# Two loads for the twiddle tables of a Fourier stage, and single moves in a written-out order

## The chip, the cores and the metric

The kernel runs on one core of one Trainium2 chip. The core has a matrix engine (TensorE, PE in the profile, with its weight loads as PEld), three engines for elementwise work (VectorE or DVE, ScalarE or ACT, GpSimd or POOL), and SyncE (SP), which here does little else than issue the transfers between the device's memory (DRAM) and the core's memory (SBUF). Matmul results are left in a third memory, PSUM, and are copied from there. The metric is the time of one execution on the device, in microseconds, as the median of several runs.

## The reference

One input x of 2048 rows and 640 columns goes through two computations, A and B, and a gate mixes them row by row:

```
g = sigmoid((x * gate_w).sum(-1, keepdims=True))
return g * A(x) + (1 - g) * B(x)
```

A is attention with a memory. There are 32 heads of 20 columns, and the rows are cut into four segments of 512. Inside a segment each head does ordinary causal softmax attention. Beside it the head reads a memory matrix M and a sum z, both built from the keys and values of earlier segments, with phi(t) = t + 1 for positive t and exp(t) otherwise:

```
a_mem = (phi(q) @ M) / (phi(q) . z + 1e-6)
o = sigmoid(beta) * a_mem + (1 - sigmoid(beta)) * softmax(q k^T * scale + mask) @ v
M = M + phi(k)^T @ v ;  z = z + phi(k).sum(rows)
```

The outputs of all heads are multiplied with wo. B is a filter in the frequency domain: a two-dimensional real Fourier transform of x, a product with the complex table w_r + 1j * w_i, and the inverse transform.

## The kernel before

The kernel is a Python program that first records operations and then places them. An operation is a group of matmuls, one elementwise instruction or one transfer, with the buffers that it reads and writes and, in some cases, a choice of two engines. The order of all operations is written out by hand as one long list of numbers, ORDER: half of a number (rounded down) is the operation, and an odd number picks the second engine of its choice. The function schedule cuts the list into one queue for each engine, keeps that order, and gives out the PSUM banks; emit then writes the instructions, with a wait on a semaphore wherever an operation needs what another engine has written, or overwrites what another engine still reads. An engine works off its queue strictly in order, so an operation that waits holds up everything behind it. The table QUEUE holds planned costs of transfers; it says nothing of when they really run.

Nearly all transfers are issued by SyncE, one after another, at line 602 (plain) and line 600 (transposing). Matmuls are issued at lines 565 and 567, and copies out of PSUM at lines 577 (ScalarE) and 579 (VectorE). A transfer that waits stands in SyncE's queue as an operation stands in an engine's.

The steps that matter for the change:

- **xT, ld_x.** xT is the transposed x of a segment, a transposing load that is needed by the projections; ld_x loads plain x for the Fourier stage, where VectorE and GpSimd add and subtract halves of it first (fold, tiles xf and xsb).
- **Projections.** proj and vproj multiply xT with wq, wk and wv. Their results are copied to SBUF (ev_proj, ev_v). As a head has only 20 columns, q and k are laid out anew for the score matmuls: st_qk writes them (tile qu) to a scratch tensor qk_scr in DRAM, and pad (in the first segment pad2, in eight smaller pieces) reads them back with gaps into the tile qkp.
- **Attention.** qk (score matmuls, from qkp), exp on ScalarE (line 1357), mask on GpSimd (line 1391), pvf and pv (products with v, tile va). The results go through tiles ub and the scratch tensor u_scr (st_u, ld_u).
- **Memory.** phi of k is computed (tile phk), and a transposing transfer from SBUF to SBUF, pkT, makes the tile pkn from it, which mupd uses to update M.
- **Fourier stage.** F1 is a first transform along the rows (tile Ac); D a transform along the columns (with the table big, copied to the tile Bt by ev_D); then for each of 16 groups g come T, the forward twiddle matmuls (line 1547), W_mul, the product with the filter on VectorE (line 1548, tile Pt), W_add on VectorE or GpSimd (line 1553, tile Yt), and Tb, the inverse twiddle matmuls (line 1568), copied to the tile Cp by ev_Tb. Last come Db and Fb for the inverse transforms. The filter rows are loaded by ld_W (tile Wt), the twiddles by ld_tt (tile tt).
- **End.** final (copies to the tile ot) mixes both computations; st_out and, for the last rows, four smaller st_part write the output.

The twiddle tiles are two, tt0 and tt1, each of 128 partitions and 2048 columns. Each holds the tables of two groups, a pair: of every 1024 columns the first 512 are read by T and the other 512 by Tb. The table in DRAM has the same layout. At every even g one transfer loads a pair:

```
self.dma(lambda tt=self.tt[ti]: tt.ap(0, [1024, 2], [1, 1024]), ...,
         2 * P * 2048, [], [b("tt", ti)], early, name="ld_tt")
```

As both T and Tb name the one buffer b("tt", ti), the load of pair k waits until the last Tb of pair k - 2 is done, and T of pair k waits for the whole load. There are eight such loads. After the Fourier stage the tiles' room is used again for others; after_mid lists the buffers that must be free by then.

TensorE works the array in three shapes: the whole array (projections, Fourier stage), tiles of 20 rows by 64 columns (qk), and tiles of 128 rows by 32 columns (pv, vproj in part, the output product). Along TensorE's queue the shape changes 206 times.

Of the kernel before, what the change touches and what calls it, by code (L numbers as in the profile page):

```python
# [510 lines left out]
class Kern:  # L511
# [84 lines left out]
    def dma(self, dst, src, nbytes, r, w, prio, tr=False, name="", after=(), queue="sp"):  # L596
# [24 lines left out]
        ("ld_big", 329728): (500.0, 950.0, 16, 1000.0), "ld_inv": (500.0, 1400.0, 16, 1000.0), ("ld_tt", 262144): (400.0, 1300.0, 16, 250.0), ("ld_tt", 524288): (400.0, 1750.0, 16, 600.0),  # L621
# [218 lines left out]
    def after_mid(self, key):  # L840

        if key in self.seen:
            return []
        self.seen.add(key)
        b = self.b
        return ([b("tt", i) for i in range(self.NT)] + [b("Wt", i, r, h) for i in range(2) for r in range(2) for h in range(2)] +
                [b("Bt", i, r) for i in range(2) for r in range(2)] + [b("Yt", i, r) for i in range(2) for r in range(2)] +
                [b("Pt", i, r, q) for i in range(2) for r in range(2) for q in range(2)])

# [878 lines left out]
```

## Time and profile before

| What | us |
|---|---|
| median of 3 runs (lowest, highest) | 234.89 (234.76, 235.56) |
| the profiled execution | 236.6 |
| its span | 234.5 |
| TensorE busy | 225.3 |
| VectorE busy | 190.0 |
| ScalarE busy | 194.6 |
| GpSimd busy | 148.3 |

The span is the time from the first to the last instruction on the core; the execution has 2.1 us around it. The granted clock of TensorE is full in all slices of the profile. Matmuls are pipelined and the ends that the profile gives for them are modelled, so a TensorE that is busy is not thereby at its best; what can be read well is when each matmul starts.

A row of a list of waits names the waiting engine and line, then behind the arrow who released it, and then the total of the waits, how many there were and the longest, in us. A row of a chain or of a timeline begins with a start and a length in us. SPq is SyncE issuing a transfer: its length is the time that the issue took, not the transfer, which lands later. A row of a tile gives the shortest, median and longest duration in ns and the first and the last start in us.

### The profile page before, as it was taken

The page shows a single profiled execution, that of the slowest core. Times are in us where ns is not written, and L with a number is a line of the kernel's source. Part 1 is how long each engine was busy: PE and PEld are TensorE (multiplying, and loading weights), DVE is VectorE, ACT ScalarE, POOL GpSimd, SP SyncE. Part 2 cuts the span into 40 slices and gives each one's busy share as a digit, 9 for nine tenths or more (in the row PEclk, how much of TensorE's full clock was granted, in tenths as well). Part 3 has the DMA queues.
Part 4 walks back from the last instruction along what each step waited for, and adds up shares of the span by engine and source line. Part 5 has one row for each costly group of instructions (what it writes and reads, how often), then busy time and mean ns, then how long its engine had stood idle before and what let it go on. Part 6 is the DMA issues. An engine that isn't in the chain of part 4 may idle for free.

```text
span 234.5 us, 10377 instructions
## 1 busy us (share of the span) xinstructions
PE 225.3 (96%) x4395; PEld 141.9 (61%) x4395; DVE 190.0 (81%) x485; ACT 194.6 (83%) x216; POOL 148.3 (63%) x301
## 2 busy tenths in 40 slices
PE   7899999999999999999999999999999998999994
PEld 2575576676547666654557555555645466767793
DVE  0189897889999998799999898999799983955364
ACT  2189797789999999999999989999999898788720
POOL 8233127456768875567775869478998768387700
PEclk9999999999999999999999999999999999999999
DMA  7999955998989978556893755685899752222524
GB/s 149 279 338 209 251 165 142 192 234 219 259 200 188 193 192 243 140 157 180 217 210 95 241 173 130 190 194 182 227 166 196 203 152 81 76 77 59 180 95 122
DMA packets 59265, 42.18 MB, mean 180 GB/s; under 512 B 30228, under 2 KB 55380, under 8 KB 59220
## 3 DMA queue, kind: packets, MB, share of 16 engines
q1 hardware_dynamic: 58180, 40.96, 70.3%
q8 instruction: 34, 0.56, 1.1%
q10 hardware_dynamic: 1040, 0.57, 1.0%
q14 instruction: 11, 0.09, 0.2%
HBM read 23.32 MB, written 12.30 MB: 152 GB/s over the span
## 4 chain that ended last, share of the span: by engine, by line
PE 69%; DVE 10%; DMA 8%; ACT 5%; SPq 4%; issue 2%; POOL 1%; DVEq 0%; ACTq 0%
PE psum L567 64%; PE psum L565 5%; DMA out_dram<-ot 4%; SPq L602 4%; ACT ex L1357 3%; DVE Pt L1548 3%; DMA xT<-in_A_x_dram 2%; DMA qk_scr<-qu 1%; DVE Cp L579 1%; DVE G L1602 1%; ACT ub L577 1%; DVE Bt L579 1%; DVE Yt L1553 1%; POOL ex L1391 1%; POOL Yt L1553 1%
## 5 line engine op out<-in xcount | busy, mean ns | idle before, releaser
L1357 ACT ACTIVATE ex<-psum 128x2048 bf16<-128x2048 f32 (+1 forms) x73 | 135.2, 1853 | 10.7 <-PE psum L567 9.5
L1391 POOL TENSOR_SCALAR_AFFINE_SELECT ex<-ex 128x256 bf16<-128x256 bf16 (+3 forms) x224 | 104.5, 484 | 42.0 <-ACT ex L1357 10.9
L567 PE MATMUL psum<-xT,wk 128*128 128x256 bf16 (+1 forms) x280 | 33.3, 273 | 0.2 <-DVE mem L1229 0.2
L567 PE MATMUL psum<-qkp 20*64 20x64 bf16 (+5 forms) x1280 | 31.9, 270 | 1.3 <-ACT ex L1357 0.7
L567 PE MATMUL psum<-xT,wq 128*128 128x512 bf16 (+1 forms) x135 | 31.9, 380 | 0.9 <-DMA xT<-in_A_x_dram 0.9
L567 PE MATMUL psum<-wv,xT 128*32 128x321 bf16 (+3 forms) x385 | 28.0, 301 | 0.1
L1548 DVE TENSOR_TENSOR Pt<-psum,Wt 128x642 bf16<-128x642 f32 x32 | 25.4, 814 | 0.5 <-PE psum L567 0.3
L567 PEld LDWEIGHTS psum<-qkp 20*64 20x64 bf16 x1280 | 13.7, 103 | 17.2 <-ACT ex L1357 11.2
L567 PEld LDWEIGHTS psum<-xT,wk 128*128 128x128 bf16 (+1 forms) x280 | 20.0, 97 | 6.4 <-issue 1.8
L977 POOL TENSOR_TENSOR xsb<-xf 128x320 bf16<-128x320 bf16 (+2 forms) x11 | 8.1, 744 | 20.7 <-DVE xf L972 11.0
L565 PE MATMUL psum<-wo,oU 128*32 128x320 bf16 x460 | 19.6, 299 | 0.0
L567 PE MATMUL psum<-big,Cp 128*128 128x321 bf16 (+1 forms) x96 | 18.8, 303 | 0.1
L1187 DVE TENSOR_TENSOR va<-psum,ebx 128x320 bf16<-128x320 f32 x32 | 14.9, 483 | 4.4 <-PE psum L567 2.0
L567 PEld LDWEIGHTS psum<-wv,xT 128*32 128x32 bf16 (+1 forms) x385 | 13.4, 96 | 7.1 <-issue 1.5
L567 PE MATMUL psum<-ex,va 128*32 128x64 bf16 (+3 forms) x576 | 17.2, 256 | 0.2
L567 PE MATMUL psum<-big,Ac 128*128 128x161 bf16 (+2 forms) x96 | 17.1, 257 | 0.2
L567 PE MATMUL psum<-tt,Yt 128*128 128x256 bf16 (+1 forms) x96 | 16.4, 275 | 0.4 <-POOL Yt L1553 0.3
L1602 DVE TENSOR_TENSOR G<-eo,psum 128x320 bf16<-128x320 f32 x32 | 14.9, 482 | 1.8 <-PE psum L567 1.3
L567 PEld LDWEIGHTS psum<-ex,va 128*32 128x32 bf16 x576 | 10.9, 96 | 8.7 <-POOL ex L1391 0.7
L1144 ACT ACTIVATE et<-qu 128x512 bf16<-128x512 bf16 x25 | 15.4, 625 | 0.2 <-DVE phq L1157 0.2
L972 DVE TENSOR_TENSOR xf<-xsb 128x640 bf16<-128x640 bf16 x16 | 7.9, 501 | 8.5 <-DMA xsb<-in_A_x_dram 8.4
L579 DVE CAST Bt<-psum 128x322 bf16<-128x322 f32 x26 | 13.2, 516 | 2.0 <-PE psum L567 1.8
(102 smaller groups left out, 394.0 us busy)
## 6 DMA issues: line engine op xcount, KB each, us to landing
qkp<-qk_scr SPq DMA_DIRECT2D x28, 160.0 KB
tt<-tab_tt SPq DMA_DIRECT2D x8, 512.0 KB, 5.7
qk_scr<-qu SPq DMA_DIRECT2D x12, 256.0 KB, 3.5
u_scr<-ub SPq DMA_DIRECT2D x12, 256.0 KB, 4.2
xsb<-in_A_x_dram SPq DMA_DIRECT2D x8, 320.0 KB, 5.6
oU<-u_scr SPq DMA_DIRECT2D x15, 128.0 KB, 3.2
out_dram<-ot SPq DMA_DIRECT2D x12, 160.0 KB
Wt<-in_B_w_r_dram SPq DMA_DIRECT2D x16, 80.2 KB, 4.1
```

The lines of the kernel that those rows point to most:

```text
L565: h = e.matmul(dst, wt, r_, start=st, stop=sp_, **{**kw, "tile_position": (0, q), "skip_group_check": True})
L567: h = e.matmul(o_, l_, r_, start=st, stop=sp_, **kw)
L579: alts["dve"] = (lambda e: e.tensor_copy(dst(), src()), 67 + 1.04 * n, 68.0)
L602: return e.dma_start(d_, s_)
L972: self.either(lambda e, r=r, op=op: e.tensor_tensor(xf.ap(r * 642, [321, 2], [1, 320]), xs.ap(o, [D, 2], [1, 320]), xs.ap(o + 320, [D, 2], ...
L977: self.either(lambda e, dst=dst, src=src, d0=d0, n=n, op=op: e.tensor_tensor(xs.ap(o + dst, [D, 2], [1, n]), xf.ap(src + d0, [321, 2], [1, ...
L1144: self.one("act", lambda e: e.activation(et.ap(0, [1, L]), qsl(), ACT.Exp), L, [qb], [b("et", pi_)], late, fix=95, name="phi_exp")
L1187: self.one("dve", lambda e: e.tensor_tensor(va.ap(i * H * VW + h0 * VW, [VW, nh], [1, DH]), self.ps(bank, 0, [DH, nh], [1, DH]), self.ebx. ...
L1357: self.one("act", lambda e, d=d, q=q: e.activation(self.ex.ap(*d), self.ps(bank, *q), ACT.Exp, scale=SC), 2048 if kind < 2 else 512 * n, [ ...
L1391: self.one("pool", lambda e: e.affine_select(self.ex.ap(*d, p0=p0, np_=np_), self.ex.ap(*q, p0=p0, np_=np_), [[0, 4], [1, n]], ALU.is_ge, ...
L1548: self.one("dve", lambda e, ri=ri, Pt=Pt, Wt=Wt, wo_=wo_, bank=bank: e.tensor_tensor(Pt.ap(ri * 322, [644, 2], [1, KD]), self.ps(bank, 0, ...
L1602: self.one("dve", lambda e, q=q, n2=n2, bank=bank, eo=eo: e.tensor_tensor(self.G.ap(n2 * D + 639 * q, [1 - 2 * q, 320]), eo.ap(q, [1, 320] ...
```

## The change

The load of a pair becomes two: ld_tt loads the columns of T (512 of every 1024, 256 KB) and ld_tp those of Tb. They write two separate buffers, b("tt", ti, 0) and b("tt", ti, 1), in the same tile; T reads the first only and Tb the second only. So ld_tt of pair k waits for the last T of pair k - 2, and ld_tp for its last Tb. A row of the transfer is 1 KB rather than 2 KB. The matmuls, the table in DRAM and the rooms in SBUF stay as they are.

```diff
-                self.dma(lambda tt=self.tt[ti]: tt.ap(0, [1024, 2], [1, 1024]), lambda g=g: dap(self.tab["tt"].ap(), g * P * 1024, [1024, P], [P * 1024, 2], [1, 1024]),
-                         2 * P * 2048, [], [b("tt", ti)], early, name="ld_tt")
+                for part, name in enumerate(("ld_tt", "ld_tp")):
+                    self.dma(lambda tt=self.tt[ti], part=part: tt.ap(512 * part, [1024, 2], [1, 512]),
+                             lambda g=g, part=part: dap(self.tab["tt"].ap(), g * P * 1024 + 512 * part, [1024, P], [P * 1024, 2], [1, 512]),
+                             2 * P * 1024, [], [b("tt", ti, part)], early, name=name)
...
-                self.mms(items, [b("tt", ti), b("Bt", g % 2, 0), b("Bt", g % 2, 1), bank], [], prio2, name="T", mode=0)
+                self.mms(items, [b("tt", ti, 0), b("Bt", g % 2, 0), b("Bt", g % 2, 1), bank], [], prio2, name="T", mode=0)
...
-                    self.mms(items, Yb + [b("tt", ti), bank], [], prio3, name="Tb", mode=0)
+                    self.mms(items, Yb + [b("tt", ti, 1), bank], [], prio3, name="Tb", mode=0)
```

after_mid lists both parts, and QUEUE gets a planned cost for ld_tp. The rest of the diff is ORDER. Its numbers shift because eight operations are new; read back as queues, these are the moves:

- **SyncE.** Near the start, two xT go up: one in front of another xT, one in front of two ld_x. The order of some st_qk changes. pkT of the first segment, which stood behind the eight pad2, stands behind the first of them; the st_qk that follows the pkT before now follows the last pad2. One ld_W goes up among the pads behind them, and another st_qk of the second segment too; the first ld_tp goes behind these pads, ahead of ld_big and of the first ld_tt. The second ld_tp stands six places behind its ld_tt, the third ten, behind a st_u and a st_qk; the fourth to the eighth stand directly behind theirs. In the second and third segment several ld_W, a ld_gc (a load of gate values) and a st_u change places; one pad, which before was issued between a st_o and an xT, goes down behind a later st_qk, ahead of the fourth ld_tt, together with a small load (ld_den). Further on, one ld_wo goes up, one ld_u goes ahead of a st_r, and of the four st_part two change places.
- **TensorE.** Ten groups of matmuls change places: single proj, qk, pvf, pv, vproj, Db and output groups go a few places up or down. The shape of the array changes 203 times rather than 206.
- **VectorE and ScalarE.** Some fold, phi, ev_proj, ev_v, W_add, mem and ev_Tb steps change places with neighbours on VectorE. One final goes from ScalarE to VectorE.
- **GpSimd.** One zeroing step and one gate step go down.

More of the change, by code (lines that the diff above doesn't have):

```diff
@@ L620 @@
         ("ld_W", 41088): (600.0, 250.0, 16, 450.0), ("ld_W", 82176): (600.0, 500.0, 16, 550.0), ("ld_big", 659456): (500.0, 1750.0, 16, 950.0),
-        ("ld_big", 329728): (500.0, 950.0, 16, 1000.0), "ld_inv": (500.0, 1400.0, 16, 1000.0), ("ld_tt", 262144): (400.0, 1300.0, 16, 250.0), ("ld_tt", 524288): (400.0, 1750.0, 16, 600.0),
+        ("ld_big", 329728): (500.0, 950.0, 16, 1000.0), "ld_inv": (500.0, 1400.0, 16, 1000.0), ("ld_tt", 262144): (400.0, 1300.0, 16, 250.0), ("ld_tp", 262144): (400.0, 1300.0, 16, 250.0), ("ld_tt", 524288): (400.0, 1750.0, 16, 600.0),
         ("ld_u", 131072): (595.0, 650.0, 16, 450.0), ("ld_u", 655360): (595.0, 1700.0, 16, 1800.0), ("ld_u", 262144): (595.0, 1000.0, 16, 900.0),
@@ L845, in after_mid @@
         b = self.b
-        return ([b("tt", i) for i in range(self.NT)] + [b("Wt", i, r, h) for i in range(2) for r in range(2) for h in range(2)] +
+        return ([b("tt", i, p) for i in range(self.NT) for p in range(2)] + [b("Wt", i, r, h) for i in range(2) for r in range(2) for h in range(2)] +
                 [b("Bt", i, r) for i in range(2) for r in range(2)] + [b("Yt", i, r) for i in range(2) for r in range(2)] +
```

190 rows, old and new, of the table ORDER are left out of this document.

## The prediction

> **What bounds the kernel now.** I read the page first, for the shares; then TensorE's list of waits, for what it lost and to whom; then the chain of work that ended last, by stretches, for where a saved wait would arrive at the end; and last the timelines of TensorE and of the DMA queue around the moved steps.
>
> ```profile
> span 234.5 us, 10377 instructions
> ...
> PE 225.3 (96%) x4395; PEld 141.9 (61%) x4395; DVE 190.0 (81%) x485; ACT 194.6 (83%) x216; POOL 148.3 (63%) x301
> ```
>
> TensorE is busy in 225.3 of 234.5 us. At most 9 us are open to any change that leaves its matmuls alone, as this one does.
>
> ```profile
> PE psum L567 <- DVE G L861: 1.3, 1, 1.3
> ...
> PE psum L567 <- DMA tt<-tab_tt: 0.3, 1, 0.3
> ```
>
> In this list of waits (total, times, longest) the twiddle table tt, which the change splits, appears once and with 0.3 us: of the eight loads of the table only one was late for TensorE. That is the whole direct gain.
>
> ```profile
> 37.23 3.43 DMA qk_scr<-qu
> ...
> 40.74 0.69 DVE qu L579
> 41.44 0.41 DVE va L1187
> ...
> 41.89 3.11 PE psum L567 x52
> ```
>
> This is the chain between 37 and 45 us (start, length, what). A store of q/k to scratch was issued at 37.23, landed 3.43 later, and the copy to qu on VectorE could only then overwrite the buffer; TensorE went on at 41.89. So the chain there runs through the DMA queue and its issue order, which the change edits.
>
> ```profile
> 131.50 1.01 POOL ex L1391 x2
> ...
> 132.57 0.41 POOL ex L1391
> 132.98 0.70 POOL Yt L1553
> ...
> 133.99 1.56 DVE Pt L1548 x2
> ...
> 135.59 6.96 PE psum L567 x128
> ...
> 180.90 0.39 SPq L602
> ...
> 189.81 4.38 DMA out_dram<-ot
> 194.27 0.45 ACT ot L577
> ...
> 194.76 0.32 PE psum L567 x4
> ```
>
> These are two later stretches. At 131 to 135 us, where the tt wait lies, the chain does not name the tt load: it goes over the causal masks on GpSimd and the twiddle products on VectorE. From 180.90 to 194.76 it is the DMA queue: a row of issues, then an output store that landed 4.38 after its issue, then a copy on ScalarE that had to wait for that store's buffer. What TensorE saves between 181 and 194 is waited out again at 194.76.
>
> **The change part by part.** *The split.*
>
> ```profile
> L567 PE MATMUL psum<-tt,Yt x96: 269/273/299, 60.0 to 162.1; 128*128 128x256 bf16 x64, 128*65 128x256 bf16 x32
> L567 PE MATMUL psum<-Bt,tt x64: 297/302/311, 53.5 to 155.9; 128*128 128x321 bf16 x64
> L602 SPq DMA_DIRECT2D tt<-tab_tt x8: 379/474/1111, 48.0 to 148.8; - x8
> ```
>
> The matmuls keep their number and shapes; 8 issues become 16. The new ones cost the queue 8 x 0.474 = 3.8 us in all. A new issue delays its neighbours by 0.47 us until the queue next idles, and the inverse part is not wanted until 6.2 to 6.5 us after the forward part (60.0 - 53.5 at the first pair, 162.1 - 155.9 at the last). The third pair's inverse half stands furthest down, ten issues behind its forward half and behind two stores; it is the one that could come late. I take 0 for the eight issues and for the second loads; if the cover goes, one late neighbour costs TensorE 0.47.
>
> What the split frees is pair 5 (the sixth load).
>
> ```profile
> 124.53 0.61 SPq L602 DMA_DIRECT2D Wt<-in_B_w_r_dram  x1
> 127.22 0.39 SPq L602 DMA_DIRECT2D tt<-tab_tt  x1
> ```
>
> ```profile
> 131.69 0.24 PE L567 MATMUL psum<-big,Ac 128*128 128x161 bf16 x1
> 132.21 0.44 PE L567 MATMUL psum<-Bt,tt 128*128 128x321 bf16 x2 [0.28 <-DMA tt<-tab_tt]
> 132.58 1.28 PE L567 MATMUL psum<-ex,va 128*32 128x512 bf16 x48
> ```
>
> The queue stood idle from 125.14 to 127.22, since the buffer was still read by the last inverse matmul of pair 3. In the changed kernel the forward half waits only for the last forward matmul of pair 3, long past, so it can go at 125.2, 2.0 us sooner, and with the same 5.0 us to the matmul that used it (127.22 to 132.21) it is there at 130.2, ahead of 131.93, where TensorE began to wait. The 0.28 goes. What is late next is the mask in the chain above: it ends at 132.51 before the matmuls at 132.58 can start, in the chain's rows 131.50 + 1.01, though its part that those need may end sooner. So the gain lies between 0 and 0.28. I take 0.25, the end that the wait itself shows, because two forward matmuls (0.44) are done before the mask rather than beside it, and VectorE's products come behind them.
>
> A rule speaks against the split. The Trainium skill (DMA: Bandwidth & Descriptors, "Rules for kernel authors") says to coalesce many small transfers into one large, and under "Anatomy of one DMA" fits 2.0 us fixed plus bytes at 436 GB/s for a DMA issued by GpSimd. By that fit, an estimate, 512 KB take 3.2 us and two loads of 256 KB in series 5.2, 2.0 more; the 0.28 would stay a wait if the forward half came second. No run here shows the price of the halves yet; the forward half is issued first.
>
> *The transposing loads of x at the start (xT), two of them moved up the queue, past plain loads of x.*
>
> ```profile
> 26.34 0.38 PE L567 MATMUL psum<-xT,wk 128*128 128x256 bf16 x2
> 26.73 0.80 PE L567 MATMUL psum<-wv,xT 128*128 128x320 bf16 x3
> ```
>
> ```profile
> 19.39 2.91 SPq L600 DMA_TRANSPOSE xT<-in_A_x_dram  x2
> ```
>
> Two groups of v-projection matmuls started as those transposes landed. Three such matmuls take 0.59 where nothing is waited for (a row of this shape at 41.21 stands below); these took 0.80, so 0.20 was lost inside. Two of 256 columns begin about 0.11 apart (320 columns: 0.14), so they need 0.22 of the 0.39 from 26.34 to 26.73: 0.17 lost, 0.37 together. Both transposes now go at least one issue (0.5 us) sooner, so I take all 0.37 as saved by 27 us. The plain loads behind them go 0.5 to 1.5 us later; their folds on VectorE feed matmuls after 31 us; cost 0, or at most the 0.37 again.
>
> *The transposing load of the keys (pkT) moved from behind eight small loads of padded k (pad2) to behind the first.*
>
> ```profile
> 30.99 4.88 SPq L602 DMA_DIRECT2D qkp<-qk_scr  x8
> 35.92 1.21 SPq L600 DMA_TRANSPOSE pkn<-phk  x1
> ```
>
> ```profile
> 37.37 0.42 PE L567 MATMUL psum<-qkp 20*64 20x320 bf16 x16 [0.26 <-DMA qkp<-qk_scr]
> ```
>
> TensorE's first score matmuls waited for the last of the eight: issued by 35.87, used at 37.37. Seven of them now stand behind a 1.21 us transpose, so the last is up to 1.21 + 0.1 later. Less is possible: eight such issues at the queue's shortest take 8 x 0.37 = 3.0, they took 4.88, so about 1.9 us in there was a stall of the queue itself; whatever stands in the queue during it costs nothing. The view of the DMA queues names one other user that the engines' own progress sets off:
>
> ```profile
> q8 instruction: 34, 0.56, 1.1%
> ```
>
> These 34 transfers are instruction loads; I assume the stall is one of them, and TensorE's, as its program is the longest. The transpose can lie in the stall; then the loads still to come after it are six instead of four, 0.75 more, and if the stall is tied to TensorE it comes 0.37 sooner. So between 0 and +1.3; I take 0.75 - 0.37 = +0.4. The 0.37 from the start is gone here in every case: TensorE waits longer instead, to an end which the DMA sets.
>
> *What the same move frees.* The store at 37.23 stood behind that transpose; it now goes right behind the loads, at 36.3 to 36.9 us. The chain 37.23, 40.74, 41.44, 41.89 starts 0.4 to 0.9 sooner. TensorE's own row there:
>
> ```profile
> 41.21 0.59 PE L567 MATMUL psum<-wv,xT 128*128 128x320 bf16 x3
> ```
>
> Three matmuls in 0.59, of about 0.31 each, begin 0.14 apart, so a next one could begin at 41.63; it began at 41.89. That 0.26 goes: -0.26 (bounds 0 and -0.26). Behind that store stand four larger pads, and a filter load (0.61, as at 124.53) and a store (0.37, as at 91.66 below) now go among them: 0.98 more against the 1.21 that left, so 0 for them, and late only if the small loads are late by over a microsecond. Net of the two at 42 us: +0.4 - 0.26 = +0.14, from -0.26 to +1.3.
>
> *One load of padded k (pad) moved far down, behind the store at 91.66.*
>
> ```profile
> 91.66 0.37 SPq L602 DMA_DIRECT2D qk_scr<-qu  x1
> 92.07 0.48 SPq L602 DMA_DIRECT2D tt<-tab_tt  x1
> ```
>
> ```profile
> tt<-tab_tt SPq DMA_DIRECT2D x1, 512.0 KB, 5.7
> qk_scr<-qu SPq DMA_DIRECT2D x1, 256.0 KB, 4.8
> ```
>
> ```profile
> 97.30 0.58 PE L567 MATMUL psum<-qkp 20*64 20x64 bf16 x48
> ```
>
> It is issued at 92.07 and wanted at 97.30. With the 4.8 of its neighbour it lands at 96.9, with 5.7 at 97.8. I take 0 (it is the smallest of the three transfers), with +0.5 as the far end.
>
> *Matmul order.* Ten matmul groups change places, with three fewer changes between array shapes (206 to 203), one fewer near 50 us and the rest inside 184 to 194 us or at 21 us. No row shows one by itself. The row at 131.69 has ended at 131.93 and the wait behind it hides the next change, so I bound a change between nothing and 0.14, the distance of two matmuls of 320 columns: between 132.21 + 0.44 and the group of another shape at 132.58 there is no idle at all, so what a change costs lies inside the matmuls' own times. I take -0.1 for the one near 50; those at 184 to 194 go into the wait that ends at 194.76.
>
> *Tail.* One combination step goes from ScalarE to VectorE around 222 us; both have idle time there. Two of the last stores change places.
>
> ```profile
> 230.85 0.90 DVE ot L579 x2
> ```
>
> ```profile
> 230.91 1.81 SPq L602 DMA_DIRECT2D out_dram<-ot  x4
> ```
>
> The first row is the end of the chain: the last combination ends at 230.85 + 0.90 = 231.75, and of the four issues (0.45 each) at least one must follow it. The last store to land may go by up to one issue sooner, 0 to -0.45; I take -0.1, nearer to nothing, since no store can go before 231.75. The other moves (weights W, gates, masks, copies) shift work by less than a microsecond beside engines that are not waited for: 0, between -0.3 and +0.5.
>
> **Sum:** +0.14 - 0.25 - 0.1 - 0.1 = -0.31 on the profiled execution's 236.6 us (its span of 234.5 and 2.1 around it): 236.3. That execution is 1.7 above the median of the runs, 234.89, so I put the same difference on the median: 234.6.
>
> **The rivals.**
> *Keys late (slower).* The transpose goes ahead of the stall, not into it, and all of its 1.21 + 0.1 comes on the last small load: +1.3 - 0.26 at 42 us, with the late pad at 97.30 +0.2: total +1.3 - 0.26 + 0.2 - 0.45 = +0.8, 235.7. For it: the small loads are already the last thing that TensorE waits for, by 0.26, with no slack. Against: 1.9 us of stall in the same place. It decides as soon as the last small load is issued more than about 1.2 later.
> *All gains arrive (faster).* The transpose vanishes in the stall and the last small load is not later: -0.26 at 42, -0.28 at 132, -0.45 at the tail, -0.1: -1.1, 233.8. For it: each wait is in the records. Against: the chain at 131 to 135 does not name the tt load.
> *Hidden anyway (the split does nothing).* The mask, not the table, releases 132.58 and 135.59: the 0.25 falls away; with the +0.14 and -0.2 it is -0.06, 234.8.
> *The pair costs more than the one.* 3.8 us more issuing, of which one neighbour each in the dense stretches before 100 us and in the row of issues 180.90 to 189.77 lands late, 0.47 twice: -0.31 + 0.94 = +0.6, 235.5. Against it: no added issue lies in 180.90 to 189.77 (the last new load is before 150 us), so at most the first half is real, and then it is 235.1. It is the case in which the rule on coalescing, quoted above from the Trainium skill, would hold.
>
> **How the numbers follow.** From no change 0.3%, 0.7 us, can be told. The sum as it stands: 0.35, 234.6, no measurable change. All gains: 0.28, faster. Keys late: 0.21, slower. Hidden anyway: 0.11, no change. The pair costs more: 0.05, split evenly between no change (235.1) and slower (235.5, at the border). The sum's own errors reach over the border on the faster side more often than on the other (its bounds reach -1.1 with the tail): I move 0.09 from it to faster. That makes faster 0.37, no change 0.39, slower 0.24. The range takes in "all gains" (233.8) with 0.2 below for the small moves, and "keys late" (235.7): 233.6 to 235.8. The likeliest's own range is 234.2 to 235.3.
>
> **What would show it.** The split: no wait for tt in TensorE's list, and a tt issue near 125.2. The start: the v-projection group at 26.7 without its 0.20, and a wait for qkp near 37 longer than 0.26, 0.6 to 1.1. The store: TensorE past 41.89 with no gap and no store of q/k in the chain at 37 to 41. The late pad: no wait for qkp at 97. The end: the store and copy at 189 to 194.7 shifted with all the rest, not longer. The prediction is wrong if the wait near 37 exceeds 1.3, if a new DMA wait shows between 85 and 100, or if VectorE's chain from 151 to 161 takes up what was gained before it.

## The result and the profile after

The changed kernel takes 238.23 us as the median of five runs (237.40 to 238.94); the kernel before took 235.08 beside it (234.76 to 235.86). The ratio is 1.0109 with a 95% interval of 1.0071 to 1.0148: about 2.6 us slower. A later measurement of the same kernel (after_again) gave 236.73 against 235.58, 1.0067 (1.0041 to 1.0093). Ratios here compare only the runs in the chip's fast state, by an estimate that isn't the quotient of the two medians (that would be 1.0134 and 1.0049). So the kernel is slower by both measures, and whether by 0.7% or by 1.1% is open. The forecast was 234.6.

The profiled execution took 237.81 us with a span of 235.8. That is only 1.3 above the span of before, since that execution of before lay above its own median and this one below its own. In the pair of traces, then, some 1.3 us can be followed and not all of the 2.6. The first rows of the page (span; busy time, share and count of each engine):

```profile
span 235.8 us, 10377 instructions
...
PE 223.5 (95%) x4381; PEld 141.5 (60%) x4395; DVE 191.2 (81%) x486; ACT 193.9 (82%) x215; POOL 148.8 (63%) x301
```

The kernel has the same matmuls as before, but this trace lacks 14 of their records: 4381 matmuls stand beside 4395 weight loads. So its 223.5 can't be set beside the 225.3 of before. The trace of after_again, the same kernel, has all of them:

```profile
PE 226.2 (96%) x4395; PEld 141.5 (60%) x4395; DVE 190.4 (81%) x486; ACT 193.9 (82%) x215; POOL 148.7 (63%) x301
```

What was lost is therefore read from the list of waits and from the starts of the matmuls. The list, in part (who released TensorE: total, times, longest):

```profile
PE psum L567 <- DVE G L861: 1.3, 1, 1.3
PE psum L567 <- issue: 0.9, 4, 0.3
...
PE psum L567 <- DMA pkn<-phk: 0.8, 1, 0.8
...
PE psum L567 <- DVE va L1187: 0.7, 1, 0.7
PE psum L567 <- DMA qkp<-qk_scr: 0.6, 1, 0.6
```

The wait for tt is gone, as forecast. Two waits for transfers, pkn and qkp, and one for VectorE's copy to va stand there instead. (Some short waits that are left out, as one of 0.3 for Pt, stand where records are missing: that one is in all nine traces of this document with 4381 matmuls and in none of the nine with 4395.) TensorE's timeline shows where (in brackets: the idle time before the row and who ended it):

```profile
26.11 0.57 PE L567 MATMUL psum<-wv,xT 128*128 128x320 bf16 x3
...
28.68 0.40 PE L567 MATMUL psum<-fcat,xsb 128*128 128x128 bf16 x4 [0.69 <-DVE va L1187]
...
37.40 0.42 PE L567 MATMUL psum<-qkp 20*64 20x320 bf16 x16
...
41.74 0.28 PE L567 MATMUL psum<-fcat,xsb 128*128 128x128 bf16 x2
...
45.03 0.58 PE L567 MATMUL psum<-qkp 20*64 20x64 bf16 x48 [0.59 <-DMA qkp<-qk_scr]
...
47.25 0.43 PE L567 MATMUL psum<-va,pkn 128*128 128x154 bf16 x4 [0.76 <-DMA pkn<-phk]
```

Set beside the starts of the same matmuls before (26.73 and 37.37 in the prediction; the last two rows stand below), this is a ladder. TensorE is 0.6 ahead at 26, as the move of xT was to bring. At 37.40 it is level; the lead is used up, and so is the wait of 0.26 that stood there before. Then it falls behind, by 0.5 at 45.03 and by 1.4 at 47.25. The timeline of before at the last two:

```profile
44.53 0.58 PE L567 MATMUL psum<-qkp 20*64 20x64 bf16 x48
...
45.83 0.43 PE L567 MATMUL psum<-va,pkn 128*128 128x154 bf16 x4
```

There neither group waited. By 50 us the lag is 1.8. The last part of it comes with a pause of 0.24 before 50.13, for which the profile shows no wait; late_pad, an experiment below without these moves, has one of 0.55 in the same group of matmuls. Later the lag lies between 1.0 and 2.3, and at the end it is 1.3. It rises once more by 0.3, at the first scores that read the pad which was moved far down:

```profile
99.57 0.58 PE L567 MATMUL psum<-qkp 20*64 20x64 bf16 x48 [0.27 <-issue]
```

The row names no releaser, but by the updates of its semaphore the late pad, issued at 94.64, landed at 99.48. Most of what stays arises before 50 us, ahead of the first matmul that reads a twiddle table (55.3 in the changed kernel). The chain of the changed kernel goes through the transfers there (start, length, what):

```profile
19.14 4.64 DMA xsb<-in_A_x_dram
23.81 0.04 DVE xf L972
...
28.22 0.41 DVE va L1187
28.68 7.11 PE psum L567 x122
...
41.90 5.22 DMA pkn<-phk
47.12 0.14 issue
47.25 2.63 PE psum L567 x63
```

The chain shows two places. At 19 to 28 us a plain load of x, issued at 19.14 and landed 4.64 later, holds VectorE's folds and with them the copies to va that stand behind the folds. At 42 to 47 us it is the transposing load of the second keys. This is SyncE's timeline ahead of it:

```profile
36.57 0.71 SPq L602 DMA_DIRECT2D qkp<-qk_scr  x2
37.32 1.76 SPq L602 DMA_DIRECT2D Wt<-in_B_w_r_dram  x1
39.12 0.52 SPq L602 DMA_DIRECT2D qkp<-qk_scr  x1
39.69 0.48 SPq L602 DMA_DIRECT2D qk_scr<-qu  x1
40.22 0.52 SPq L602 DMA_DIRECT2D qkp<-qk_scr  x1
40.78 0.38 SPq L602 DMA_DIRECT2D tt<-tab_tt  x1
41.20 0.65 SPq L602 DMA_DIRECT2D Wt<-in_B_w_r_dram  x1
41.90 1.33 SPq L600 DMA_TRANSPOSE pkn<-phk  x1
```

A filter load, a store and the first ld_tp now stand between or behind the four pads and ahead of the pkT. The pads are needed at 45.03, the pkT at 47.25. One issue alone, a filter load's, took 1.76 us; most of its kind take 0.5 to 0.7.

Further down the split does what it says. Tile tt in the changed kernel (shortest, median, longest in ns; first and last start in us):

```profile
L567 PE MATMUL psum<-Bt,tt x64: 298/302/311, 55.3 to 157.8; 128*128 128x321 bf16 x64
L602 SPq DMA_DIRECT2D tt<-tab_tt x16: 369/472/2307, 40.8 to 150.7; - x16
```

Sixteen issues of the same median length as the eight before (the longest took 2.3 us, against 1.1), and no T waits for any of them.

### The profile page after: what moved, and what is told of

It reads as the page before. It is cut to its first block, busy times and chain, and to the rows that moved or that the text cites. A ratio compares the mean times of both kernels' runs of the same rounds, so it can differ in the third digit from the quotient of the medians.

```text
span 235.8 us, 10377 instructions
## 1 busy us (share of the span) xinstructions
PE 223.5 (95%) x4381; PEld 141.5 (60%) x4395; DVE 191.2 (81%) x486; ACT 193.9 (82%) x215; POOL 148.8 (63%) x301
## 4 chain that ended last, share of the span: by engine, by line
PE 65%; DVE 14%; DMA 8%; SPq 5%; ACT 5%; issue 2%; POOL 0%; DVEq 0%
PE psum L567 58%; PE psum L565 8%; DMA xsb<-in_A_x_dram 5%; ACT ex L1357 4%; SPq L600 3%; DVE Pt L1550 3%; DMA pkn<-phk 2%; SPq L602 2%; DVE Cp L579 1%; DVE G L1604 1%; DVE mem L1229 1%; DVE Bt L579 1%; DVE phk L1157 1%; DVE xf L972 1%; DVE Yt L1555 1%
## 5 line engine op out<-in xcount | busy, mean ns | idle before, releaser
L567 PE MATMUL psum<-xT,wq 128*128 128x512 bf16 (+1 forms) x121 | 27.9, 380 | 1.4 <-DMA xT<-in_A_x_dram 0.6
L972 DVE TENSOR_TENSOR xf<-xsb 128x640 bf16<-128x640 bf16 x16 | 8.4, 531 | 9.9 <-DMA xsb<-in_A_x_dram 9.9
```

What stands on the lines that cost most here:

```text
L567: h = e.matmul(o_, l_, r_, start=st, stop=sp_, **kw)
L972: self.either(lambda e, r=r, op=op: e.tensor_tensor(xf.ap(r * 642, [321, 2], [1, 320]), xs.ap(o, [D, 2], [1, 320]), xs.ap(o + 320, [D, 2], ...
```

## The experiments

Runs sent together share a chip and the runs of the kernel before, so ratios of one group are compared first of all within it.

### The parts apart

split_only is before with the split alone: each ld_tp directly behind its ld_tt in SyncE's queue, all else in the order of before. moves_only is the changed order on all engines with one load per pair.

```diff
 split_only, SyncE's queue
  ld_tt (pair k)
+ ld_tp (pair k)
 moves_only
  ORDER of the changed kernel, its eight ld_tp left out; one ld_tt per pair as before
```

> The split alone: the order of before on every engine, with each second load (ld_tp) directly behind its first (ld_tt). Theory 'places' (the loss comes from where transfers were put in SyncE's queue, not from the split): the wait for tt at 132 goes, 0.3 to 0.4 us, and nothing else moves: 234.7 against 235.1 for the kernel before. Rival 'halves' (two loads of 1 KB rows cost more than one of 2 KB rows, and eight more issues hold up the queue): slower than before by 0.5 us or more, up to the 2.6 us by which the changed kernel is slower.

> The moves alone: the order of the changed kernel on every engine, but one load for each pair, at the place of ld_tt, as before. 'Places': the loss stays but for what ld_tp added ahead of the second pkT (about 0.4 us), and the wait at 132 is back (0.4): 237.5 to 238.2. 'Halves': 235.0 to 235.5, the loss is gone.

split_only 236.54, 1.0033 (1.0005 to 1.0061); moves_only 237.40, 1.0076 (1.0041 to 1.0111), both against 235.70. The moves cost the more, and the split does not come out free either, though by its edit it adds only issues. Then SyncE's part of the moves and the engines' part:

```diff
 sp_moves: SyncE's queue in the changed order, all other queues as before; one load per pair
 eng_moves: SyncE's queue as before, all other queues in the changed order; one load per pair
```

> The kernel before with SyncE's queue in the changed order and nothing else: one load for each pair, all engines in the order of before. 'Places' (the moves in SyncE's queue carry the loss of the moves, 0.76 percent): 1.005 to 1.009 of the kernel before. Rival 'engines' (the moves on the engines carry it): 0.998 to 1.003.

> The kernel before with TensorE, VectorE, ScalarE and GpSimd in the changed order, and SyncE's queue as before. 'Places': 0.997 to 1.002 of the kernel before. 'Engines': 1.005 to 1.009. If both halves of the moves cost about 0.4 percent the two theories share it.

sp_moves 238.52, 1.0125 (1.0079 to 1.0172); eng_moves 235.73, 1.0007 (0.9972 to 1.0041), both against 235.26. The moves on the engines are worth nothing that can be told; the loss lies in the order of SyncE's queue. The execution of sp_moves that was profiled has a short drop of the granted clock near 205 (last section), which lengthens its span; its waits before 50 us are read without regard to it.

### Which moves in the queue

x_back puts the loads at the start back into the order of before; pads_back does so around the four larger pads of the first segment, with ld_tp directly behind the first ld_tt; both_back does both.

```diff
 x_back, start of SyncE's queue
- xT, xT, ld_x, xT, ld_x, st_qk, ld_x, ld_x
+ xT, ld_x, ld_x, ld_x, xT, xT, ld_x, st_qk
 pads_back, after the eight pad2
- st_qk, pad, pad, ld_W, pad, st_qk, pad, ld_tp, ld_W, pkT, ld_W, ld_W, xT, st_qk, ld_W, ld_big, ld_tt, hm
+ st_qk, pad, pad, pad, pad, ld_W, pkT, st_qk, ld_W, ld_W, xT, st_qk, ld_W, ld_big, ld_tt, ld_tp, hm
```

> The changed kernel with the transposed and the plain loads of x at the start in the order of before. 'Places': VectorE no longer stands idle for 1.7 us at 22 to 24 and the stall of TensorE at 28 (0.7 by its starts, 1.0 against the kernel before) goes. But what TensorE gains there it waits for again at 45 and 47, where the pads and pkn land by the queue's own time: I expect 0.2 to 0.6 us less than the changed kernel, 237.4 to 237.8; the whole 1.0 only if those landings come earlier too. 'Engines': no change, 237.9.

> The changed kernel with three transfers put back behind the pads and the second pkT of the first segment: one ld_W, one st_qk and the first ld_tp. 'Places': the waits of 0.65 at 45.0 (qkp) and 0.92 at 47.3 (pkn) go, and perhaps the 0.4 at 50 with them: 1.6 to 2.0 us less than the changed kernel, 236.0 to 236.5. Rival 'engines' (the loss comes from the moves on TensorE, VectorE and GpSimd): no change from the changed kernel, 237.9.

> The changed kernel with the loads of x at the start and the three transfers ahead of the second pkT both put back. 'Places', if those two are all of it: the stalls at 28, 45 and 47 go, 2.0 to 2.6 us less than the changed kernel, 1.000 to 1.003 of the kernel before. If the loss sits elsewhere too (each of the two alone gave back less than its stalls): 1.004 to 1.009.

x_back 1.0062 (1.0027 to 1.0097) and pads_back 1.0106 (1.0048 to 1.0163) against 235.70; both_back 237.04, 1.0078 (1.0042 to 1.0114) against 235.26. Beside the 1.0109 of the changed kernel x_back may be worth some 0.4%; pads_back is worth nothing, although its trace had neither wait at 45 and 47. By the theory that the pads carry the loss it should have been faster, so something in pads_back costs as much as the waits that went. It shares a trait with split_only: the ld_tp directly behind the first ld_tt.

### What the place of one load does

split_by_group splits the table in the other way, by group: two loads of 256 KB with rows of 2 KB.

```diff
- tt.ap(512 * part, [1024, 2], [1, 512]) <- g * P * 1024 + 512 * part, [1024, P], [P * 1024, 2], [1, 512]
+ tt.ap(1024 * part, [1, 1024]) <- (g + part) * P * 1024, [1024, P], [1, 1024]
- T reads b("tt", ti, 0), Tb reads b("tt", ti, 1)
+ T and Tb of group g read b("tt", ti, g % 2)
```

> The kernel before with each pair's load cut in two by group rather than by stage: two loads of 256 KB with rows of 2 KB, one for each of the two groups, each directly behind the other; forward and inverse matmuls of a group wait for their group's load. As many issues as the split alone, but no shorter rows. If the split's 0.33 percent comes from the rows of 1 KB: 0.997 to 1.001 of the kernel before. If it comes from eight more issues in dense stretches of the queue: 1.002 to 1.006, like the split alone.

236.16, 1.0040 (1.0007 to 1.0072), not to be told from split_only. Rows of 2 KB do not help, so nothing shows that the split's cost lies in rows of 1 KB. The traces of both show what may be: GpSimd's timeline in split_by_group, and then in split_hm (below) at the same place:

```profile
55.51 0.51 POOL L1469 TENSOR_TENSOR Mz<-Macc,hm 128x176 bf16<-128x176 f32 x1
...
57.29 0.42 POOL L1391 TENSOR_SCALAR_AFFINE_SELECT ex<-ex 128x256 bf16<-128x256 bf16 x1 [1.27 <-DVE phk L1156]
```

```profile
53.12 0.51 POOL L1469 TENSOR_TENSOR Mz<-Macc,hm 128x176 bf16<-128x176 f32 x1
53.59 0.41 POOL L1391 TENSOR_SCALAR_AFFINE_SELECT ex<-ex 128x256 bf16<-128x256 bf16 x1
```

A mask step on GpSimd stands 1.27 us and waits for a step of VectorE with which it shares no data. The program puts that wait there itself: schedule reckons a time for every step from the planned costs in QUEUE, and where by this reckoning a step on GpSimd follows one on VectorE, it adds a wait for it. In the same reckoning it gives out the PSUM banks. A load put one place higher shifts the planned times, and with them three such waits and the banks of about a thousand operations. split_hm moves only that load, one place down:

```diff
 split_only -> split_hm, SyncE's queue, pair 0
  ld_tt
- ld_tp
  hm
+ ld_tp
```

This leaves waits and banks as they were before.

> The split alone as before, but with the first ld_tp one place further down, behind the small load of the mask table hm. Theory 'inserted wait': with the first ld_tp directly behind ld_tt, the kernel's own scheduler (it simulates the order with planned costs and adds waits from those times) made one mask step on GpSimd at 55 us wait for a VectorE step that ends 2 us later; here it adds no wait and picks no PSUM bank other than in the kernel before. So the idle of GpSimd near 55 and the 1.0 us that TensorE lost at 58 to 61 go, and the wait for tt at 132 stays gone: 0.996 to 0.999 of the kernel before. Rival 'issues' (eight more issues cost by themselves): 1.002 to 1.006, as the two splits before.

235.65 against 235.20, 1.0024 (0.9990 to 1.0059): the difference from no change is not shown, but the gain that was expected is not there, and the value lies in the range given to the rival, that eight more issues cost something by themselves. The mask's wait is gone, and TensorE, which lost 0.8 us at 58 to 61 in split_by_group, loses nothing there. The traces show the wait and its absence; the ratios (1.0033, 1.0040, 1.0024) do not separate the kernels. The trace of split_hm, of an execution that took 237.52, has a wait of 1.75 for another pkn at 75.53; that pkT was issued no later than before (70.41 against 70.79), and no other trace has this wait. The sharper test is pads_back with the same correction. Its added waits and its banks are those of the changed kernel. Where the x loads go back too (both_back_hm, and x_back), the added waits stay the same, but 558 of 1546 operations get other banks:

```diff
 pads_back -> pads_back_hm, SyncE's queue, pair 0 (both_back -> both_back_hm alike)
  ld_tt
- ld_tp
  hm
+ ld_tp
```

> The changed kernel with the ld_W and the st_qk put back behind the pads and the second pkT, and the first ld_tp behind hm instead of ahead of that pkT: unlike the earlier try, no wait is added and no PSUM bank differs from the changed kernel. 'Places': the waits at 45.0 and 47.3 go and nothing comes back at 58 to 61: 1.000 to 1.006 of the kernel before, 1.2 to 1.9 us less than the changed kernel. If those waits were an accident of one execution: 1.009 to 1.013, like the changed kernel.

> As the last, with the loads of x at the start in the order of before too. 'Places': what the moves of the loads of x cost by themselves (0.37 percent) goes as well: 0.996 to 1.002 of the kernel before. If a third place in SyncE's queue costs as much: 1.003 to 1.008, as in the earlier try with both put back.

> The changed kernel once more, on the chip of these runs. 'Places': 1.008 to 1.013 of the kernel before, and in its trace again a stall of TensorE at 28 behind VectorE's folds, and a wait for pkn or qkp at 45 to 47. If the stalls of the first trace were one execution's: other places in this one.

All three against 235.58: the changed kernel 1.0067 (1.0041 to 1.0093), pads_back_hm 236.47, 1.0028 (0.9997 to 1.0058), both_back_hm 235.31, 1.0009 (0.9984 to 1.0034). Now the steps come out in order: putting the transfers around the pads back takes 0.4%, putting the x loads back another 0.2%, and nothing that can be told is left. The intervals of neighbours overlap; those of the first and the last do not. So the two moves together are shown to carry the loss, the second of them with the banks that change with it, and how it is shared is not shown: by the medians (236.73, 236.47, 235.31) the x loads would have the larger part. One more pair differs in the transfers around the pads alone, with the same added waits and banks: x_back with 1.0062 and both_back_hm with 1.0009, in two groups, with intervals that just overlap. And both_back_hm keeps every other move of the change and the split, so all these together cost at most 0.34%. TensorE's timeline, after_again first, then pads_back_hm:

```profile
29.10 0.40 PE L567 MATMUL psum<-fcat,xsb 128*128 128x128 bf16 x4 [0.75 <-DVE va L1187]
...
45.25 0.58 PE L567 MATMUL psum<-qkp 20*64 20x64 bf16 x48 [0.31 <-DMA qkp<-qk_scr]
...
47.25 0.43 PE L567 MATMUL psum<-va,pkn 128*128 128x154 bf16 x4 [0.55 <-DMA pkn<-phk]
```

```profile
43.54 0.58 PE L576 MATMUL psum<-qkp 20*64 20x64 bf16 x48
...
44.84 0.43 PE L576 MATMUL psum<-va,pkn 128*128 128x154 bf16 x4
```

The three waits come again in a second execution of the changed kernel, at the same places. Without the inserted transfers there is none at 43.54 and 44.84. SyncE's timeline of pads_back_hm shows the queue:

```profile
35.59 1.53 SPq L611 DMA_DIRECT2D qkp<-qk_scr  x4
37.17 0.73 SPq L611 DMA_DIRECT2D Wt<-in_B_w_r_dram  x1
37.95 2.18 SPq L609 DMA_TRANSPOSE pkn<-phk  x1
```

From the first of the four pads to the issue of the pkT it is 2.36 us (37.95 - 35.59) instead of 5.33 (41.90 - 36.57). Not all of that is due to the three inserted transfers. In each of these executions one issue there takes about a microsecond more than its like: the filter load in the changed kernel (1.76), a pad in after_again (1.18) and the pkT itself in pads_back_hm (2.18, against 1.33). Each time one of the 34 instruction loads that the prediction found in the profile (queue q8) is under way, from 36.96, 39.48 and 37.72 on. So the long issue is not a cost of the insertion. Counted past it, from the first pad's issue to the landing of the pkT, it is 10.5 us in the changed kernel (41.90 + 5.22 - 36.57), 10.1 in after_again and 8.4 in pads_back_hm (37.95 + 6.0 - 35.59): about 2 us more. At their usual lengths the three issues take 1.6 of this (0.72 + 0.48 + 0.38 in after_again).

The other traces narrow this. The wait for this pkn is there in all three traces with all three transfers inserted (the two of the changed kernel; 0.57 in x_back) and in no other; moves_only and sp_moves, which have the filter load and the store there but no ld_tp, are without it. The wait for qkp at 45 comes in other orders too (0.67 in x_only, 0.39 in best), so only part of it is the inserted transfers' doing. And since this execution of pads_back_hm is the fastest of its twelve (234.34) and its whole queue also ran earlier, the trace alone would not prove the step; it is the traces and the ratios together that speak for it.

### The x loads, and the late pad, alone

```diff
 x_only: before with the start of SyncE's queue as in the changed kernel
- xT, ld_x, ld_x, ld_x, xT, xT, ld_x, st_qk
+ xT, xT, ld_x, xT, ld_x, st_qk, ld_x, ld_x
 late_pad: before with the one pad of the second segment moved down
- pad, xT, ..., st_qk, ld_tt (pair 3)
+ xT, ..., st_qk, pad, ld_tt (pair 3)
```

> The kernel before with the loads of x at the start in the changed order and nothing else. 'Places': the transposes land in time (no wait of the v projection at 26.7) but VectorE stands idle for the plain loads, and TensorE loses 0.6 to 1.0 us at 28 to 30: 1.001 to 1.005 of the kernel before. The prediction's step (cost 0, gain lost again at 37): 0.999 to 1.001.

> The kernel before with the one pad put in front of the fourth ld_tt (92 us) and nothing else; no other wait and no other PSUM bank. If the wait for qkp that the changed kernel shows at 97 to 99 comes from this: TensorE loses 0.2 to 0.6 us there, 1.000 to 1.003 of the kernel before. If it came from the transfers being late altogether: 0.999 to 1.001 and no wait there.

x_only 235.94 against 235.20, 1.0037 (1.0008 to 1.0066): 0.9 us from these moves alone, though here too three of the added waits differ and some 900 operations get other PSUM banks, which this run can't take apart. VectorE's list of waits from 20 to 29 us, of the changed kernel, of after_again and of x_only:

```profile
DVE xf L972 <- DMA xsb<-in_A_x_dram: 1.7, 1, 1.7
```

```profile
DVE xf L972 <- DMA xsb<-in_A_x_dram: 1.8, 1, 1.8
```

```profile
DVE xf L982 <- DMA xsb<-in_A_x_dram: 1.1, 1, 1.1
```

This row, at 0.5 to 1.8 us, is in all seven traces with the moved loads and in none of the eleven with the old order. VectorE's queue is in order, so the copies to va behind the fold come late, and for them TensorE waits at 28 to 29 us: 0.69 and 0.75 in the two traces of the changed kernel, 0.86 in sp_moves, 0.20 in x_only. In the three where VectorE lost only 0.5 to 1.0 (moves_only, pads_back, pads_back_hm) TensorE does not wait there.

late_pad 234.82 against 235.20, 0.9973 (0.9945 to 1.0001): not slower, perhaps a trifle faster. Its TensorE timeline has no wait at the scores, and shows the tt wait, for there is no split in it. So the move costs nothing by itself; in the changed order the same scores waited 0.27 in one trace of the changed kernel and 0.27 in that of sp_moves (98.36), and not in after_again (99.25).

```profile
96.99 0.58 PE L576 MATMUL psum<-qkp 20*64 20x64 bf16 x48
...
133.15 0.44 PE L576 MATMUL psum<-Bt,tt 128*128 128x321 bf16 x2 [1.19 <-DMA tt<-tab_tt]
```

### The harmless parts together

eng_split is eng_moves with the split of split_hm; best adds the late pad.

```diff
 eng_split: engines' queues as in the changed kernel; SyncE's as in split_hm
 best: eng_split
- pad, xT, ..., st_qk, ld_tt (pair 3)
+ xT, ..., st_qk, pad, ld_tt (pair 3)
```

> The moves on the engines, SyncE's queue as before, and the split with the first ld_tp behind hm. If the engines' moves are worth nothing by themselves (1.0007) and the split is worth the wait at 132 (0.4 us): 0.996 to 1.000 of the kernel before; the candidate for a kernel faster than both.

> The moves on the engines, the split with the first ld_tp behind hm, SyncE's queue otherwise as before but for the one pad moved ahead of the fourth ld_tt. The three were 1.0007, 1.0024 (0.9993 together) and 0.9973 by themselves; if they add up: 0.994 to 0.999 of the kernel before.

eng_split 235.43 against 235.20, 0.9993 (0.9963 to 1.0023); best 235.28 against 235.58, 1.0005 (0.9970 to 1.0040), where 0.994 to 0.999 was expected. Without the other moves of the queue the rest of the change costs and brings nothing that can be told: no version is shown to beat the kernel before.

## Why the prediction was wrong

The forecast of 234.6 and the range up to 235.8 failed on the moves in SyncE's queue, each of which I set at or near zero.

**The plain loads behind the xT.** The step was "The plain loads behind them go 0.5 to 1.5 us later; their folds on VectorE feed matmuls after 31 us; cost 0, or at most the 0.37 again." The first three of the second segment's plain loads do land 1.2 to 2.7 us later in the two traces of the changed kernel, the fourth at most 0.3 later. But I followed only those who read the folds, and not what stands behind the fold in VectorE's own queue: the copy to va, wanted at 28. x_only prices it at 0.37%, 0.9 us (0.2 to 1.6), other banks and added waits included. The gain set against it, 0.37 at 26 us, did arrive (26.11, and 26.47 in after_again, rather than 26.73) and was spent there.

**The transfers among the larger pads.** "0.98 more against the 1.21 that left, so 0 for them, and late only if the small loads are late by over a microsecond." This netted lengths of issues. It left out the ld_tp, and above all it looked only at the pads and not at the second pkT behind them, which falls behind all inserted transfers. The pkT lands about 2 us later against the pads than without them. The waits for qkp and pkn are 0.59 and 0.76 in one execution, 0.31 and 0.55 in the other; putting the transfers back is worth 0.4% by the ratios (0.1% by the medians).

**Waits of one execution taken as gains.** I counted 0.26 at 37, 0.26 at 41.89 and 0.37 at the start. In eng_moves, whose SyncE queue is that of before, neither score wait is in the list:

```profile
PE psum L567 <- DVE G L860: 1.3, 1, 1.3
PE psum L567 <- ACT ex L1356: 0.6, 2, 0.4
PE psum L567 <- POOL Yt L1552: 0.3, 1, 0.3
PE psum L567 <- DMA xT<-in_A_x_dram: 0.3, 1, 0.3
```

and the eight small loads were issued 2 us sooner, though nothing in SyncE's queue had changed up to there; split_hm's were too. The timelines of SyncE, eng_moves and split_hm:

```profile
28.89 4.55 SPq L602 DMA_DIRECT2D qkp<-qk_scr  x8
```

```profile
28.98 4.79 SPq L602 DMA_DIRECT2D qkp<-qk_scr  x8
```

Against 30.99 in the prediction's row. A wait of 0.3 that hangs on this queue is partly an accident of the execution it was read from.

**Not seen at all.** That an order changes the waits that schedule adds, and the banks, through its planned times. For the changed kernel these are 9 waits and the banks of 777 operations. What they cost there was not measured by itself; pads_back_hm, which has the same waits and banks and the x moves besides, bounds them all to below 0.58%.

**What was right.** The split takes the tt wait away: at 132 none is left in the twelve traces with the split (three have one of 0.2 at another T), while four of the six without it have 0.28, 0.30, 0.81 and 1.19 there. In the changed kernel TensorE's lag fell from 2.3 to 1.9 at this place, against the 0.25 that I took. The forward half was issued at 127.66, which by a TensorE that is 2.3 late there answers to 125.4, near the 125.2 named. The guess that the stall among the small loads is an instruction load fits: one was under way from 32.30 in the kernel before, and from 32.73 in the changed kernel. For the first keys +0.4 was taken; the last small load landed at 37.35 against 37.32, so it was 0 and no wait showed, while three other orders with the same move do wait there (0.37 to 0.50 in x_back, pads_back and sp_moves). The store went as forecast: no gap is left at 41.74 (41.89 before). The matmul order and the tail showed nothing.

**The late pad.** Taken at 0, with +0.5 as the far end; alone it was 0 (late_pad), but in one of two traces of the changed kernel the scores waited 0.27 for it. A new wait for a transfer between 85 and 100 was one of the prediction's own signs of being wrong, and here it stood.

**What else held.** The stretch from 181 to 196 was read rightly in the other direction: as its chain is the transfer queue's, the lag fell there from 2.0 to 1.0. What the added issues cost is not known beyond the interval of split_hm, under 0.6%, where I took 0.

Of the rivals, "keys late" had the right side and the wrong place: not the first pkT among the small loads, but the second behind the large pads. "The pair costs more" named late neighbours in the dense stretches before 100 us, as happened, but put it on the splitting. The rule of the Trainium skill that was set against the split (DMA: Bandwidth & Descriptors, "Rules for kernel authors", to coalesce) speaks of small transfers and puts the mark for mostly overhead at 64 KB. The halves here are 256 KB, so this case hardly tests it: the split by itself was not measurably slower, and 256 KB in rows of 2 KB did no better than in rows of 1 KB.

Open: how the 1.0109 of the first measurement and the 1.0067 of the second go together; why sp_moves at 1.0125 lies above moves_only at 1.0076 (their intervals overlap), and what both lose beside the x loads, since neither shows the waits at 45 and 47; how the loss is shared between the two moves, and with the banks that change beside the second; and whether the instruction loads cause the long issues beside them, which no edit tested.

## What to carry to other kernels

A transfer inserted in an in-order queue is priced by what stands behind it: find the next transfers on which an engine waits without slack, however many places down, and on the engine that waits for a delayed load look at what stands behind the waiting step. A wait of a few tenths that hangs on a busy transfer queue should be read from several executions before it is counted as a gain. Where a program derives waits and buffers from planned times, compare these before and after each edit, since moving one load by one place can add a wait between steps that have nothing in common.

## What the runs showed of the hardware

The program of split_hm is that of before on every engine up to the eight small loads, and yet they were issued from 28.98 in its trace and from 30.99 in that of before: a shift of 2 us without a change in the program up to there.

SyncE's long issues go with the instruction loads. In the eighteen traces 241 issues took over 0.5 us longer than the median of their tile, and 227 of them overlap in time with one of the 34 transfers of queue q8; with these shifted at random, about 97 would. Which transfer is held up differs between executions.

The split also makes rows of 1 KB out of rows of 2 KB; a packet of the one took 46 ns and of the other 84 (medians), so two short ones cost 92 against 84. A load of 256 KB landed 3.6 to 5.4 us after its issue, one of 512 KB 5.1 to 5.8.

The granted clock fell to one half for 3.4 us in three of the eighteen traces. In split_hm this began at 75.8, just behind the wait of 1.75, and in split_only at 63.0, just behind one of 1.74; late_pad's wait of 1.19 was not followed by it. In sp_moves it began at 203.4, with no idle time over 0.45 just before it. Its windows of 3 us there (busy us of PE, PEld, DVE, ACT, POOL, then the granted clock, the DMA share and GB/s):

```profile
200.00:203.00 3.00, 2.55 (x78) 2.07 (x75) 2.93 (x9) 2.31 (x3) 0.98 (x3) 1.00 0.28 92
203.00:206.00 3.00, 3.00 (x61) 1.63 (x61) 2.74 (x9) 2.01 (x3) 1.98 (x3) 0.57 0.15 50
```

At 0.57 the second window holds 61 matmuls, where the first had 78.
